# Two products per weight load: ordering the wq and w3 products so that the second reuses what the first has loaded

## Chip, cores, metric

The kernel runs on one core of a Trainium2 chip. The metric is device time in microseconds (us) of one execution. Times of the two kernels are compared over fast runs of the same rounds; "same" means within 2%.

## The reference, cut to what matters

One decode step of two blocks on the same token, summed: attention over a cached K and V (32 query heads, 4 KV heads, 65,536 positions, head size 128), and a small MLP mixer. All inputs are bfloat16.

```python
xn = layernorm(A_x)                                  # 1 x 1024
q = xn @ A_wq                                        # wq: 1024 x 4096
p = softmax(q @ k_cache.T * 128**-0.5); o = p @ v_cache   # 8 query heads share one KV head
h = gelu(layernorm(xn) @ w1); x1 = xn + shift(h) @ w2
h2 = gelu(layernorm(x1) @ w3) @ w4                   # w3: 1024 x 3584
out = A_x + o @ A_wo + x1 + h2
```

K and V alone are 134 MB of the 170 MB that the kernel reads, once each.

## The kernel before

Everything arrives through one DMA queue, issued by SyncE, into three slots of SBUF. First wq (slot 0), w1 and w2 (slot 1), w3 (slot 2); then K and V in eight blocks of 8.4 MB each. K block m goes to slot 0 or 2, V blocks always to slot 1. A load can be issued only when the slot's last reader is done, so three of these issues hang on the first 70 us of compute:

```python
issue(3)   # K block 0 into slot 0: after the q products have read wq
...
issue(4)   # V block 0 into slot 1: after the w1 and w2 products
...
issue(5)   # K block 1 into slot 2: after w3's products and the gelu
...
issue(6 + 2*m)   # V block m+1 into slot 1: after block m's last P*V product
```

The products that the change touches have a stationary operand of 32 equal columns (one column of the vector, broadcast) and a moving operand of 512 weights. The array of TensorE is used as four column tiles of 32 columns, each writing its own 32 partitions of PSUM, so four products can run at once (in the trace of before they start in fours, the first four within 0.01 us). For one j all four tiles hold the same column of the vector:

```python
for j in range(KT_D):               # 8 slices of the 1024 inputs
    for b in range(2):              # two PSUM banks
        for jj in range(4):         # four column tiles
            fns.append(lambda e, j=j, b=b, jj=jj: e.matmul(
                S_ps[32 * jj:32 * jj + 32, b, :], xn_bf[:, j:j + 1].broadcast_to([P, 32]),
                KV[:, 0, j * HQD + 512 * (4 * b + jj):j * HQD + 512 * (4 * b + jj + 1)],
                start=(j == 0), stop=(j == KT_D - 1), tile_position=(0, 32 * jj)))
_grp(q_pe, fns, reads=b_KV[0] + [b_xn], writes=[b_S[0], b_S[1]])
issue(3)
```

That is 64 products (line L379 of the profile), each with a weight load of its own (PEld). The same for w3 inside `proj` (line L411, third part): 56 products, seven per j, tile `k % 4`. Both stages are 16 *steps* if four products always run together: 64/4, and two steps for the seven of each j.

Of the kernel before, what the change touches and what calls it, by code (L numbers as in the profile page):

```python
# [6 lines left out]
BF = mybir.dt.bfloat16  # L7
# [109 lines left out]
def _op(q, fn, reads=(), writes=(), partial=False, loop=False):  # L117
    _deps(q, reads, writes)
    ev = q.op(fn, True, loop)
    _done(ev, reads, writes, partial)  # L120
    return ev


def _grp(q, fns, reads=(), writes=(), partial=False):
    _deps(q, reads, writes)
    ev = None
    for i, fn in enumerate(fns):
        ev = q.op(fn, i == len(fns) - 1)
    _done(ev, reads, writes, partial)
    return ev  # L130
# [16 lines left out]
def bass_parallel_sum__gqa_block_cached__mixer_s_mlp__decode_kernel(  # L147
# [31 lines left out]
    with ExitStack() as es:  # L179
# [194 lines left out]

        fns = []
        for j in range(KT_D):
            for b in range(2):
                for jj in range(4):
                    fns.append(lambda e, j=j, b=b, jj=jj: e.matmul(  # L379
                        S_ps[32 * jj:32 * jj + 32, b, :], xn_bf[:, j:j + 1].broadcast_to([P, 32]),  # L380
                        KV[:, 0, j * HQD + 512 * (4 * b + jj):j * HQD + 512 * (4 * b + jj + 1)],
                        start=(j == 0), stop=(j == KT_D - 1), tile_position=(0, 32 * jj)))
# [21 lines left out]
        def proj(s, o, ncol, vec, bank, reads, c0):  # L404
            nper = ncol // P
            nt = nper // 4
            fns = []
            for j in range(KT_D):
                for k in range(nt):
                    mv = bass.AP(KV[:].tensor, s * SLOT + o + j * ncol + 4 * k, [[kvstep, P], [nper, P], [1, 4]])  # L410
                    fns.append(lambda e, j=j, k=k, mv=mv: e.matmul(  # L411
                        S_ps[32 * (k % 4):32 * (k % 4) + 32, bank + k // 4, :], vec[:, j:j + 1].broadcast_to([P, 32]), mv,
                        start=(j == 0), stop=(j == KT_D - 1), tile_position=(0, 32 * (k % 4))))
            nbank = (nt + 3) // 4
            _grp(q_pe, fns, reads=reads, writes=b_S[bank:bank + nbank])
            for b in range(nbank):
                nb = min(4, nt - 4 * b)
                if b == 0:
                    _op(q_dve, lambda e, b=b, nb=nb: e.tensor_copy(pT_f[0:32 * nb, b, :], S_ps[0:32 * nb, bank + b, :]), reads=[b_S[bank + b]], writes=[b_pT[b]])  # L419
                else:  # L420
                    _op(q_act, lambda e, b=b, nb=nb: e.activation(pT_f[0:32 * nb, b, :], S_ps[0:32 * nb, bank + b, :], ACTF.Copy), reads=[b_S[bank + b]], writes=[b_pT[b]])
            fns = []
            for b in range(nbank):
                nb = min(4, nt - 4 * b)
                for c in range(4):
                    fns.append(lambda e, b=b, nb=nb, c=c: e.matmul(  # L426
                        M_ps[:, c0 + 16 * b + c:c0 + 16 * b + 4 * nb:4], pT_f[0:32 * nb, b, c:512:4], ident_f[0:32 * nb, 0:32 * nb:32],
                        start=(b + c == 0), stop=True, skip_group_check=True))
            _grp(q_pe, fns, reads=b_pT[0:nbank] + [b_const], writes=[b_M])

        def gelu(src_ps, width, dst_bf, b_src, b_dst):
# [7 lines left out]
            _op(q_dve, lambda e: e.tensor_tensor(out=dst_bf, in0=a_, in1=xs_, op=ALU.mult), reads=[b_misc], writes=[b_dst])  # L439

        proj(1, 0, D, xn2_bf, 2, b_w1 + [b_xn2], 256)
        gelu(M_ps[:, 256:256 + KT_D], KT_D, h1g_bf, b_M, b_h1)
        proj(1, 8 * D, D, g_bf, 3, b_w2 + [b_const], 272)
        _op(q_dve, lambda e: e.tensor_tensor(out=x1, in0=xn, in1=M_ps[:, 272:272 + KT_D], op=ALU.add), reads=[b_xn, b_M], writes=[b_x1])
        _op(q_dve, lambda e: e.tensor_tensor(out=acc[:], in0=acc[:], in1=M_ps[:, 272:272 + KT_D], op=ALU.add), reads=[b_acc, b_M], writes=[b_acc])
        issue(4)
        layer_norm(x1, b_x1, xn3, xn3_bf, b_xn3, 208)
        proj(2, 0, F, xn3_bf, 0, b_KV[2] + [b_xn3], 288)
        gelu(M_ps[:, 288:288 + KT_F], KT_F, gh_bf[:], b_M, b_gh)
        q_sp.wait_all([(q.sem, q.cnt) for q in (q_pe, q_dve, q_act, q_pool)])  # L450
# [200 lines left out]
        code = nc.m.functions[0].blocks[0].instructions  # L651
# [48 lines left out]
                nc.tensor.wait_ge(s_, v).then_inc(s_, -v)  # L700
        q_pe.emit(nc.tensor, q_pe.ops[marks[-1]:])


# [1 line left out]
_INS = ['A_x', 'A_k_cache', 'A_v_cache', 'A_wq', 'A_wo', 'B_x', 'B_w1', 'B_w2', 'B_w3', 'B_w4']  # L705
# [24 lines left out]
```

## Time and profile before

| | before |
|---|---|
| time, median of 6 runs | 400.44 us (400.36 to 400.53) |
| weight loads / products on TensorE | 1539 / 1539 |
| data queue's share of the 16 DMA engines' span | 98.7% |
| q products start, result read | 27.66, 34.21 us |
| w3 products start, result read | 58.93, 65.21 us |
| block 0 begins (first transpose of K) | 71.50 us |
| V block 1 issued / K block 1 landed | 101.21 / 108.6 us |

From the page of the kernel before: busy time per engine; the data queue (packets, MB, share of 16 engines' span); and the chain that ended last, by engine.

```profile
PE 177.8 (45%) x1539; PEld 61.1 (15%) x1539; DVE 221.3 (55%) x260; ACT 23.9 (6%) x50; POOL 7.7 (2%) x31
...
q1 hardware_dynamic: 3608, 169.87, 98.7%
...
DMA 58%; DVE 25%; PE 14%; issue 1%; ACT 1%; SPq 1%; POOL 0%
```

No compute engine is busy for much more than half of the span; the DMA engines are hardly ever idle. The next lines are the same chain in order of time (start, length, what).

```profile
27.66 6.53 PE S_ps L379 x63
...
58.93 6.26 PE S_ps L411 x43
...
71.52 37.07 DMA KV<-in_A_k_cache_dram
108.61 13.10 DVE KV L460 x3
```

The two stages that change are on the chain, but only before 71.5 us. From there on, the chain is mostly K loads and the transposes that wait for them, with w4's load at the end. The first question for such a change is therefore whether a stage before 71.5 us can move anything after it. The timeline, cut to its first 3.4 us of q products and to the end of block 0, shows the steps and the DMA issue that matters (start, length, engine; SPq is the issue itself):

```profile
27.66 0.14 PEld L379 LDWEIGHTS S_ps<-KV 128*32 128x32 bf16 x8 [1.45 <-DVE KV L359]
27.66 3.60 PE L379 MATMUL S_ps<-KV 128*32 128x512 bf16 x32 [1.36 <-DVE KV L359]
28.07 0.16 PEld L379 LDWEIGHTS S_ps<-KV 128*32 128x32 bf16 x4 [0.27 <-issue]
28.49 0.16 PEld L379 LDWEIGHTS S_ps<-KV 128*32 128x32 bf16 x4 [0.27 <-issue]
...
101.21 0.33 SPq L290 DMA_DIRECT2D KV<-in_A_v_cache_dram  x1
...
108.61 4.45 DVE L460 STREAM_TRANSPOSE KV<-KV 128x4096 f32<-128x4096 f32 x1 [6.43 <-DMA KV<-in_A_k_cache_dram]
```

Four loads every 0.43 us, always under the products of the step before. V block 1 is issued 7.4 us before K block 1 has wholly landed.

### The profile page before, as it was taken

Reading aid. Unit: us, or ns where it says so; the run is one execution under the profiler, and the core shown is the slowest. Engines: PE = TensorE matmul, PEld = TensorE weight load, DVE = VectorE, ACT = ScalarE, POOL = GpSimd, SP = SyncE. Lnnn points to the kernel's source line nnn. Section 1 sums busy time; section 2 is a strip of 40 time slices with the busy share of each in tenths; the row PEclk is TensorE's granted clock in tenths of the full one; section 3 lists DMA queues with packets and bytes.
Section 4 is the critical chain, followed back from the end, with each engine's and each line's share of the span. In section 5 each row is a group of like instructions: output and inputs, shape, how many; then the busy total and the mean of one; then the engine's idle time right before and its main releaser. Section 6 shows DMA issues by size and latency. Waiting matters only on the chain.

```text
span 399.3 us, 3500 instructions
## 1 busy us (share of the span) xinstructions
PE 177.8 (45%) x1539; PEld 61.1 (15%) x1539; DVE 221.3 (55%) x260; ACT 23.9 (6%) x50; POOL 7.7 (2%) x31
## 2 busy tenths in 40 slices
PE   0035669147134713560358036413661462147394
PEld 0022435012001110110012001100120110012232
DVE  0024230995298539843984597269647952895201
ACT  1000000011001100110011002000100110011000
POOL 5000000000000000000000000000000000000000
PEclk9998656555755665585557555855565558555979
DMA  9999899999999999999999999999999999999995
GB/s 420 420 387 487 382 441 479 440 415 427 415 427 427 433 474 433 420 427 420 433 427 433 473 433 420 421 420 433 433 433 473 433 420 420 420 433 433 416 424 219
DMA packets 3759, 169.97 MB, mean 426 GB/s; under 512 B 548, under 2 KB 552, under 8 KB 808
## 3 DMA queue, kind: packets, MB, share of 16 engines
q1 hardware_dynamic: 3608, 169.87, 98.7%
q8 instruction: 5, 0.08, 0.1%
q10 hardware_dynamic: 144, 0.00, 0.0%
q14 instruction: 2, 0.02, 0.0%
HBM read 169.87 MB, written 0.00 MB: 425 GB/s over the span
## 4 chain that ended last, share of the span: by engine, by line
DMA 58%; DVE 25%; PE 14%; issue 1%; ACT 1%; SPq 1%; POOL 0%
DMA KV<-in_A_k_cache_dram 44%; DVE KV L460 17%; DMA KV<-in_B_w_dram 8%; DMA KV<-in_A_x_dram 6%; PE S_ps L411 3%; PE OT_ps L518 3%; DVE mrow L481 2%; PE M_ps L426 2%; PE S_ps L474 2%; PE S_ps L379 2%; ACT p_sb L496 1%; DVE Yall L395 1%; PE PT_ps L505 1%; DVE pT_f L509 1%; DVE pT_f L419 1%
## 5 line engine op out<-in xcount | busy, mean ns | idle before, releaser
L460 DVE STREAM_TRANSPOSE KV<-KV 128x4096 f32<-128x4096 f32 x32 | 140.3, 4421 | 42.2 <-DMA KV<-in_A_k_cache_dram 42.2
L474 PE MATMUL S_ps<-KV,Ycur 128*32 128x512 bf16 x512 | 60.7, 623 | 126.1 <-DVE KV L460 126.1
L518 PE MATMUL OT_ps<-KV,pT_f 128*32 128x512 bf16 x512 | 46.6, 504 | 1.2 <-DVE pT_f L509 1.2
L474 PEld LDWEIGHTS S_ps<-KV,Ycur 128*32 128x32 bf16 x512 | 14.3, 126 | 158.1 <-DVE KV L460 140.5
L496 ACT ACTIVATE p_sb<-S_ps,brun 128x1024 bf16<-128x1024 f32 x16 | 17.8, 1114 | 274.7 <-DVE brun L494 174.3
L509 DVE STREAM_TRANSPOSE pT_f<-PT_ps 128x512 f32<-128x512 f32 x32 | 22.4, 701 | 14.0 <-PE PT_ps L505 14.0
L481 DVE TENSOR_REDUCE mrow<-S_ps 128x1 f32<-128x1024 f32 x16 | 19.3, 1204 | 11.3 <-PE S_ps L474 11.3
L484 PE MATMUL M_ps<-Rm,Lmat 128*128 128x16 bf16 x16 | 3.1, 194 | 38.0 <-DVE Rm L482 38.0
L505 PE MATMUL PT_ps<-p_sb,permR 128*128 128x512 bf16 x32 | 18.3, 573 | 0.8
L529 DVE SCALAR_TENSOR_TENSOR O_acc<-O_acc,ff,OT_ps 128x512 f32<-128x512 f32 x12 | 9.0, 747 | 14.4 <-PE OT_ps L518 14.4
L518 PEld LDWEIGHTS OT_ps<-KV,pT_f 128*32 128x32 bf16 x512 | 12.9, 114 | 23.6 <-issue 15.5
L411 PE MATMUL S_ps<-KV 128*32 128x512 bf16 x88 | 12.5, 571 | 2.7 <-DVE KV L359 2.7
L339 DVE CAST KV<-KV 128x8 f32<-128x8 bf16 x1 | 0.2, 172 | 22.4 <-DMA KV<-in_A_x_dram 22.4
L578 PE MATMUL S_ps<-KV,o_bf 128*1 128x512 bf16 x64 | 9.7, 476 | 4.8 <-DMA KV<-in_A_wo_dram 4.8
L484 PEld LDWEIGHTS M_ps<-Rm,Lmat 128*128 128x128 bf16 x16 | 1.7, 104 | 49.3 <-DVE Rm L482 49.3
L426 PE MATMUL M_ps<-ident_f,pT_f 64*128 64x2 f32 (+2 forms) x32 | 7.9, 372 | 2.4 <-DVE pT_f L419 2.4
L582 DVE COPY pT_f<-S_ps 1x512 f32<-1x512 f32 x1 | 0.7, 679 | 14.4 <-PE S_ps L578 14.4
L426 PEld LDWEIGHTS M_ps<-ident_f,pT_f 64*128 64x128 f32 (+2 forms) x32 | 7.7, 326 | 4.7 <-DVE pT_f L419 3.4
L419 DVE COPY pT_f<-S_ps 64x512 f32<-64x512 f32 (+1 forms) x3 | 2.1, 685 | 11.3 <-PE S_ps L411 11.3
L505 PEld LDWEIGHTS PT_ps<-p_sb,permR 128*128 128x128 bf16 x32 | 3.3, 102 | 27.2 <-ACT p_sb L496 14.7
L364 PE MATMUL M_ps<-KV 8*128 8x8 bf16 x1 | 0.2, 182 | 16.2 <-DVE Dmat_f L363 16.2
L379 PE MATMUL S_ps<-KV 128*32 128x512 bf16 x64 | 6.5, 593 | 1.4 <-DVE KV L359 1.4
(88 smaller groups left out, 88.8 us busy)
## 6 DMA issues: line engine op xcount, KB each, us to landing
KV<-in_B_w_dram SPq DMA_DIRECT2D x1, 7168.0 KB, 48.4
KV<-in_B_w_dram SPq DMA_DIRECT2D x1, 4352.0 KB, 27.4
KV<-in_B_w_dram SPq DMA_DIRECT2D x2, 2048.0 KB, 28.4
KV<-in_B_w_dram SPq DMA_DIRECT2D x1, 1792.0 KB, 31.4
KV<-in_B_w_dram SPq DMA_DIRECT2D x1, 768.0 KB, 32.8
KV<-in_B_w_dram SPq DMA_DIRECT2D x1, 256.0 KB, 32.9
KV<-in_A_k_cache_dram SPq DMA_DIRECT2D x8, 46.5
KV<-in_A_v_cache_dram SPq DMA_DIRECT2D x8, 28.0
```

Of the source, the lines that this page charges most:

```text
L379: fns.append(lambda e, j=j, b=b, jj=jj: e.matmul(S_ps[32 * jj:32 * jj + 32, b, :], xn_bf[:, j:j + 1].broadcast_to([P, 32]), KV[:, 0, j * H ...
L411: fns.append(lambda e, j=j, k=k, mv=mv: e.matmul(S_ps[32 * (k % 4):32 * (k % 4) + 32, bank + k // 4, :], vec[:, j:j + 1].broadcast_to([P, ...
L426: fns.append(lambda e, b=b, nb=nb, c=c: e.matmul(M_ps[:, c0 + 16 * b + c:c0 + 16 * b + 4 * nb:4], pT_f[0:32 * nb, b, c:512:4], ident_f[0:3 ...
L460: _op(q_dve, lambda e: e.transpose(out=KV32[:, s, o:o + 4096], in_=KV32[:, s, o:o + 4096]), reads=[b_KV[s][sub]], writes=[b_KV[s][sub]], l ...
L474: fns.append(lambda e, we=we, cm=cm, mv=mv: e.matmul(S_ps[32 * cm:32 * cm + 32, n % 4, :], Ycur[:, we, :, :].rearrange("p a g -> p (a g)") ...
L481: _op(q_dve, lambda e: e.reduce_max(mrow[:, k:k + 1], S_ps[:, 2 * k:2 * k + 2, :].rearrange("p b c -> p (b c)"), axis=AX.X), reads=b_S[2 * ...
L496: _op(q_act, lambda e: e.activation(p_sb[:, :, :].rearrange("p b c -> p (b c)"), S_ps[:, 2 * k:2 * k + 2, :].rearrange("p b c -> p (b c)") ...
L505: _op(q_pe, lambda e: e.matmul(PT_ps[:, :], permR[:, :], p_sb[:, n % 2, :], start=True, stop=True), reads=[b_p[n % 2], b_const], writes=[b ...
L509: _op(q_dve, lambda e: e.transpose(out=pT_f[:, n % 2, :], in_=PT_ps[:, :]), reads=[b_PT], writes=[b_pT[n % 2]], loop=True)
L518: fns.append(lambda e, q=q, q4=q4: e.matmul(OT_ps[32 * q4:32 * q4 + 32, g % 2, :], pT_bf[:, n % 2, q, :, 1], KV[:, s, 8192 * sub + 512 * q ...
L529: _op(q_dve, lambda e: e.scalar_tensor_tensor(out=O_acc[:, 0:512], in0=O_acc[:, 0:512], scalar=ff[:, k:k + 1], in1=OT_ps[:, k, :], op0=ALU ...
L578: _grp(q_pe, [lambda e, j=j, jj=jj: e.matmul(S_ps[32 * jj:32 * jj + 1, 1, :], o_bf[:, j:j + 1], KV[:, 0, j * D + 512 * jj:j * D + 512 * (j ...
```

## The change

Two products that use the same weights on the same column tile are made neighbours, and the second is issued without a load of its own.

```diff
         for j in range(KT_D):
-            for b in range(2):
-                for jj in range(4):
+            for jj in range(4):
+                for b in range(2):
                     fns.append(lambda e, j=j, b=b, jj=jj: e.matmul(
@@ proj: w1, w2, w3
-                for k in range(nt):
+                for k in sorted(range(nt), key=lambda k: (k % 4, k)):
@@ after the program has been emitted
+        prev, n_ld = None, 0
+        for k, i in enumerate(code):
+            if i.opcode != "Matmult":
+                continue
+            key = (i.tile_position, i.tile_size, str(i.ins[1].memref), i.ins[1].offset, str(i.ins[1].ap))
+            if key == prev and i.ins[1].dtype == BF and not i.sync_info:
+                code[k] = mybir.InstMatmult(... (cut: the same operands) ..., ldweights=False)
+                n_ld += 1
+            prev = key
+        assert n_ld > 40, n_ld
```

For q the order of tiles goes from 0 1 2 3 0 1 2 3 to 0 0 1 1 2 2 3 3; for w3 from 0 1 2 3 0 1 2 to 0 0 1 1 2 2 3. w1 and w2 have two products per j, on different tiles, and do not change. 55 loads go: 31 of q (the last product carries a semaphore and keeps its load) and 24 of w3.

## The prediction

> **What bounds the kernel now.** DMA. The queue table gives the load queue 98.7% of 16 engines' span; 169.9 MB move at 425 GB/s. The chain of waits is 58% DMA, and from 71.5 us on it runs through the K loads: the first transposes of each later block (L460) wait for a K load (42 us in all). Only before 71.5 us are the q and w3 products on a chain of compute: q products (L379) 27.66 to 34.2, w3 products (L411) 58.93 to 65.2. Even there the DMA queue stays full, because loads are issued far ahead: K block 1, issued at 71.52, starts moving only when V block 0 has landed (89).

> **What the change removes.** 55 of 1539 weight loads. One lasts about 0.146 us, but the timeline shows them running under matmuls: four matmuls start together every 0.427 us, with four loads inside. Nothing is waited for; the gain is about 0 us.

> **What it adds.** The four column tiles run at once: 64 q products take 16 steps of 0.427 us (0.216 when the clock is full), not 64. The new order puts two products of one tile in succession. They cannot overlap[...], so only the second product of one tile and the first of the next run together: two at once, not four. Weight loads still get pulled ahead ([...]the trace agrees: eight loads in the first 0.14 us, four of them past waiting matmuls).
> - q: 33 steps instead of 16. The clock rises to full at 33.5 us in this trace; 14 cold steps, then 0.216 each: end near 37.9, +3.7 us.
> - between: w1 and w2 keep their order; their luck with the clock moves, +0.3 to +1.0 us.
> - w3: three steps per j instead of two, 25 for 16: 7.9 us for 6.3, +1.7 us.
> Sum: block 0 starts near 77.2 instead of 71.5, +5.7 us (estimate, +-1 with the phase of the clock, whose full and half periods are multiples of 3.41 us in the records).

> **How much is critical.** K block 0 issue moves 34.2 to 37.9; the queue has work until 50. K block 1 issue moves to 77.2; work until 89. Both absorbed. The tight one is V block 1, issued when block 0's last PV products end: 101.2, now near 107.0 to 107.5. K block 1 lands on the first DMA engines at 106.3 and on the last at 108.6. The first load shows about 1.0 us from issue to first packet and a first packet 0.8 us longer than the later 2.42 us. So most engines idle 1 to 3 us, and the last, which sets the end, 0 to 1 us. Afterwards each later issue again has over 5 us of room. This bubble is never made up: +0.2 to +1.8 us at the end.

> **Prediction.** 401.2 us, 8 in 10 within 400.3 to 402.8. Faster by over 2%: 0.01; within 2%: 0.97; slower by over 2%: 0.02.

> **What would show it.** PEld count 1484. L379 lasts about 10 us, matmuls in pairs; L411's third part about 8. Block 0's first transpose near 77; V block 1 issued near 107; a dip of DMA share near 107 to 109, and K block 2 landing 0.3 to 2 us later than 147.3. Block 1's start stays at 108.6. If no dip: 400.4.

> **What would make it wrong.** If a weight load cannot pass the second product of the previous pair, each step grows by about 0.1 us, block 0 slips some 11 us, and the bubble reaches 5 us (406). If a tile accepted its second product without waiting, nothing moves. If the DMA engines' lags even out differently, the bubble counts fully (+2 to +3 us).

The premise of "two at once, not four" was that products start in program order. No trace shows the premise; it was an assumption of mine. Block 0's +5.7 us is +3.7 for q, +1.7 for w3 and +0.3, the low end of what stands for w1 and w2.

## The result, and the profile after

| | before | after |
|---|---|---|
| time, median of 6 runs | 400.44 us (400.36 to 400.53) | 400.48 us (400.33 to 400.66) |
| weight loads / products recorded | 1539 / 1539 | 1484 / 1523 |
| q: start, result read, length | 27.66, 34.21, 6.55 us | 27.53, 32.58, 5.05 us |
| w3: start, result read, length | 58.93, 65.21, 6.28 us | 57.91, 63.16, 5.25 us |
| block 0 begins | 71.50 us | 69.50 us |
| V block 1 issued / K block 1 landed | 101.21 / 108.6 us | 99.84 / 108.2 us |

The ratio is 1.0001, interval 0.9988 to 1.0014: the same. The 16 products that after lacks are missing from the trace, not from the program: they are of L505, which the page of after counts 16 times instead of 32. All 64 of L379 and all 88 of L411 are there.

The chain of after, in order of time, with the lines that answer to those above:

```profile
27.53 5.03 PE S_ps L379 x64
...
57.91 5.23 PE S_ps L411 x34
...
69.47 38.72 DMA KV<-in_A_k_cache_dram
108.21 13.10 DVE KV L460 x3
```

Both stages got *shorter*, not longer, and the wait for K block 1 that follows took up nearly all of it: 38.72 us for 37.07. The timeline of after:

```profile
27.53 0.12 PEld L379 LDWEIGHTS S_ps<-KV 128*32 128x32 bf16 x4 [1.45 <-DVE KV L359]
27.53 3.69 PE L379 MATMUL S_ps<-KV 128*32 128x512 bf16 x40 [1.36 <-DVE KV L359]
27.93 0.16 PEld L379 LDWEIGHTS S_ps<-KV 128*32 128x32 bf16 x4 [0.28 <-issue]
28.78 0.16 PEld L379 LDWEIGHTS S_ps<-KV 128*32 128x32 bf16 x4 [0.69 <-issue]
29.64 0.16 PEld L379 LDWEIGHTS S_ps<-KV 128*32 128x32 bf16 x4 [0.69 <-issue]
30.40 0.11 PEld L379 LDWEIGHTS S_ps<-KV 128*32 128x32 bf16 x4 [0.60 <-issue]
...
99.84 0.33 SPq L290 DMA_DIRECT2D KV<-in_A_v_cache_dram  x1
```

Four loads now come every second step: 27.93 to 28.78 is 0.85 us, two times 0.427. Half of the loads are gone, and the length of a step is what it was. The start of every single product is in the trace (us; "+" marks one beside which a load starts, within 5 ns):

```
before  27.663+ 27.667+ 27.670+ 27.673+ | 28.065+ 28.068+ 28.072+ 28.074+ | 28.492+ 28.494+ 28.498+ 28.501+
after   27.530+ 27.535+ 27.540+ 27.545+ | 27.929+ 27.935+ 27.941+ 27.946+ | 28.355  28.362  28.368  28.373
```

This was not in the prediction: four start together, although the program says tile 0, tile 0, tile 1, tile 1. A load that starts beside a product is mostly not that product's own, but one pulled ahead for the tile's next weights. In before the first group has eight loads, four of its own and four (27.677 to 27.687 us) for the second group; three of these four have passed a product that still waits (the prediction says four). In after the second group are the second products of the four tiles, which have no loads of their own: the loads at 27.93 are for the next j, whose products are the third group. e2 below shows the same on one tile alone, with a load beside every second product. (The trace does not name the tile of a product. That the four are of four tiles follows from e2 too, where products of one tile never start closer than one step, 0.427 us before the clock goes up and 0.216 us after it.)

Why was the stage 1.5 us shorter, then? Count the steps in the trace: 16 in both kernels, for q and for w3 alike. What differs is when the granted clock went up (in w3 of before the record has 0.50 up to 64.21 us and 1.00 from there, and the steps go from 0.427 to 0.219 us): steps of 0.427 us become steps of 0.216 us at 33.49 us in the trace of before, 5.83 us after the first product, and at 30.30 us, 2.77 us after it, in that of after. The experiments show the same relation (table under e1), and a check there says that it is not the change.

### The profile page after: what moved, and what is told of

It reads as the page before. It is cut to its first block, busy times and chain, and to the rows that moved or that the text cites. A ratio compares the mean times of both kernels' runs of the same rounds, so it can differ in the third digit from the quotient of the medians.

```text
span 399.1 us, 3429 instructions
## 1 busy us (share of the span) xinstructions
PE 168.9 (42%) x1523; PEld 59.0 (15%) x1484; DVE 221.4 (55%) x260; ACT 23.9 (6%) x50; POOL 7.7 (2%) x31
## 3 DMA queue, kind: packets, MB, share of 16 engines
q1 hardware_dynamic: 3608, 169.87, 98.7%
## 4 chain that ended last, share of the span: by engine, by line
DMA 59%; DVE 25%; PE 12%; issue 1%; ACT 1%; SPq 1%; POOL 0%
DMA KV<-in_A_k_cache_dram 45%; DVE KV L460 18%; DMA KV<-in_B_w_dram 8%; DMA KV<-in_A_x_dram 6%; PE S_ps L411 3%; PE OT_ps L518 2%; DVE mrow L481 2%; PE M_ps L426 2%; PE S_ps L474 2%; PE S_ps L379 1%; ACT p_sb L496 1%; DVE Yall L395 1%; DVE pT_f L509 1%; DVE pT_f L419 1%; PE PT_ps L505 0%
## 5 line engine op out<-in xcount | busy, mean ns | idle before, releaser
L460 DVE STREAM_TRANSPOSE KV<-KV 128x4096 f32<-128x4096 f32 x32 | 140.3, 4422 | 44.3 <-DMA KV<-in_A_k_cache_dram 44.3
L411 PE MATMUL S_ps<-KV 128*32 128x512 bf16 x88 | 12.1, 538 | 2.7 <-DVE KV L359 2.7
L505 PE MATMUL PT_ps<-p_sb,permR 128*128 128x512 bf16 x16 | 9.7, 607 | 0.8
L505 PEld LDWEIGHTS PT_ps<-p_sb,permR 128*128 128x128 bf16 x32 | 3.3, 102 | 27.5 <-ACT p_sb L496 14.7
```

What stands on the lines that cost most here:

```text
L411: fns.append(lambda e, j=j, k=k, mv=mv: e.matmul(S_ps[32 * (k % 4):32 * (k % 4) + 32, bank + k // 4, :], vec[:, j:j + 1].broadcast_to([P, ...
L460: _op(q_dve, lambda e: e.transpose(out=KV32[:, s, o:o + 4096], in_=KV32[:, s, o:o + 4096]), reads=[b_KV[s][sub]], writes=[b_KV[s][sub]], l ...
L505: _op(q_pe, lambda e: e.matmul(PT_ps[:, :], permR[:, :], p_sb[:, n % 2, :], start=True, stop=True), reads=[b_p[n % 2], b_const], writes=[b ...
```

## The experiments

Theory A: a load costs nothing because it runs under the products in flight, and a product that waits for its own tile does not hold back the other tiles; and what happens before block 0 moves the end only when V block 1 is issued too late. Rivals: B, products start strictly in program order (the assumption behind the prediction); C, loads do cost, and either the new order hides it or the room before the DMA does. All eleven kernels of the experiments gave the correct result.

### e1: the new order, all loads kept

```diff
 (the change's two new orders stay)
-        prev, n_ld = None, 0
-        for k, i in enumerate(code): ... ldweights=False
```

> The order of the change, with every weight load kept. Theory A (loads lie hidden under the four products in flight, and a product that waits for its own column tile does not hold back the products of other tiles): the q products start four together, every 0.427 us with the half clock and every 0.216 us with the full clock, 64 loads, and the time is 400.4 +-0.3 us, as before and as with the change. Theory B (my prediction: products start strictly in program order): pairs of two, 33 steps. Theory C (the removed loads are what kept the changed order from costing time): with the loads back, the steps grow above 0.427 and 0.216 us.

Measured: 400.51 us, ratio 1.0000 (0.9984 to 1.0017). All 64 loads are there, eight in the first step and four in each later one but the last, and the 64 products go in 16 steps of 0.427 and 0.216 us. A holds; B falls; C in the form "the missing loads pay for the order" falls.

With the length of q set beside the moment at which the steps change from 0.427 to 0.216 us (both from the trace), five kernels fall on one line. With T the time from the first product to that moment, 16 steps take T + (16 - T/0.427) x 0.216, and about 0.2 us pass from the end of the last step to the reader (0.22 in before, 0.24 in after):

| kernel | loads of q | T, us | by the formula | q length, us |
|---|---|---|---|---|
| after | 33 | 2.77 | 5.0 | 5.05 |
| e1, new order, all loads | 64 | 3.35 | 5.3 | 5.35 |
| e4, old order, half the loads | 33 | 4.58 | 5.9 | 5.93 |
| before | 64 | 5.83 | 6.5 | 6.55 |
| e3, runs of four, half the loads | 33 | 5.95 | 6.6 | 6.67 |

The formula is an estimate from the two step lengths. Neither the number of loads nor the order appears in it. Whether they move T itself has to be asked: in the three runs with q in pairs T was short (2.77, 3.35 and 3.65 us in after, e1 and r8_after), and in the four with q in the old order long (4.58 to 5.83 us in e4, r2, r8_before and before). The w3 stage answers it: in pairs and with the same loads left out, its clock went up 3.11 us after its first product in after and 5.29 us in e3; in the old order of before it was 5.28 us. So one order has both, and the short times of q in pairs are chance as far as these traces show. In the traces of before and after the granted clock goes to and fro between 1.00 and 0.50, and each whole stretch lasts 1 to 10 times 3.41 us (before: 1.00 from 33.49 to 36.90, 0.50 to 47.14, 1.00 to 50.56, 0.50 to 64.21 us). The rise in q came at no fixed time from the kernel's start: 30.30 us in after, 30.96 in e1, 31.95 in e4, 33.44 in e3, 33.49 in before (first product plus T). Here that makes 1.6 us of difference between stages that do the same (5.05 to 6.67 us). A stage comparison on one profile each would have credited the change with it.

### e2: sixteen in a row on one tile

```diff
-        for j in range(KT_D):
-            for jj in range(4):
+        for jj in range(4):
+            for j in range(KT_D):
                 for b in range(2):
```

> The q products ordered tile by tile: sixteen in a row on one column tile (eight weights, each used twice), then the next tile. Counts steps of one product time. Theory A with a short queue for each tile (depth d of products waiting): about 16 + 3 x (15 - d) steps, so about 58 for d = 1, 46 for d = 5. Theory A without a limit: 16 steps, four together from the start. Theory B (strict program order): about 61 steps, hardly ever two at once.

Measured: 49 steps; q took 13.17 us; 403.43 us (one look; before, on the same chip, 400.39 to 400.66). Loads of q in the timeline, from the start and from where the second tile joins:

```profile
27.37 0.10 PEld L379 LDWEIGHTS S_ps<-KV 128*32 128x32 bf16 x1 [1.45 <-DVE KV L359]
27.77 0.15 PEld L379 LDWEIGHTS S_ps<-KV 128*32 128x32 bf16 x1 [0.30 <-issue]
28.63 0.15 PEld L379 LDWEIGHTS S_ps<-KV 128*32 128x32 bf16 x1 [0.70 <-issue]
...
31.19 0.15 PEld L379 LDWEIGHTS S_ps<-KV 128*32 128x32 bf16 x1 [0.70 <-issue]
32.04 0.81 PEld L379 LDWEIGHTS S_ps<-KV 128*32 128x32 bf16 x5 [0.70 <-issue]
33.19 0.10 PEld L379 LDWEIGHTS S_ps<-KV 128*32 128x32 bf16 x1 [0.34 <-issue]
```

The starts of the products show 11 steps with one product each, then 5 steps with two, then 6 with one, 5 with two, and so on. So products of one tile go one at a time, and the next tile begins when the one before it has four products still waiting: 16 + 3 x 11 = 49. The order does matter; it only has to be much worse than that of the change.

This run also tests the other half of the prediction, because it delays everything by as much as I had predicted for the change: block 0 begins at 77.59 us and V block 1 is issued at 107.01 (predicted: near 77.2, and 107.0 to 107.5). The DMA view between 104 and 112 us, first of before, then of e2, there with the issue of V block 1 from its timeline:

```profile
DMA packets 65, 3.21 MB, mean 401 GB/s; under 512 B 16, under 2 KB 16, under 8 KB 16
...
q1 hardware_dynamic: 65, 3.21, 93.3%
```

```profile
107.01 0.33 SPq L290 DMA_DIRECT2D KV<-in_A_v_cache_dram  x1
...
DMA packets 51, 2.29 MB, mean 287 GB/s; under 512 B 16, under 2 KB 16, under 8 KB 16
...
q1 hardware_dynamic: 51, 2.29, 73.9%
```

There is the bubble: by the trace's DMA packets the 16 engines idle about 1.9 us in the mean between 100 and 113 us, and 0.0 us in before. K block 1 lands on time (108.05) and block 1 begins on time, but V block 1 lands at 130.0 instead of 127.9 and everything behind it stays late. The time grew by 2.95 us over the 400.48 of before (one look). The prediction's mechanism for a late issue is right; its size, +0.2 to +1.8 us, was too small, and the case it listed under what would make it wrong ("the bubble counts fully (+2 to +3 us)") is what happened.

### e3: runs of four on one tile

```diff
-        for j in range(KT_D):
-            for jj in range(4):
+        for j0, jj, dj in [(j0, jj, dj) for j0 in range(0, KT_D, 2) for jj in range(4) for dj in range(2)]:
+            for j in [j0 + dj]:
                 for b in range(2):
```

> The q products in runs of four on one column tile (two j, each twice). If one waiting product per tile is all that can be held (d = 1): about 34 steps in place of 16, two tiles at a time. If d is 3 or more: 16 steps, as before. Strict program order: about 49 steps.

Measured: 16 steps, four products together from the first on; 400.38 us (one look). In its first step nine products of tiles 0 to 2 wait while tile 3's first product has already started. So the limit seen in e2 is not on all waiting products together but on those of one tile. Its trace happens to have the clock of before (T 5.95 us), and then all its times agree with before's: block 0 begins at 71.47 us for 71.50.

### e5 and e6: runs of eight, with and without the loads

e5 is e3 with groups of four j in place of two (runs of eight); e6 is e5 without the part that drops loads.

> The q products in runs of eight on one tile. If each tile holds four waiting products (as the 49 = 16 + 3 x 11 steps of runs of sixteen suggest): the next tile starts three steps after the last, 29 steps in all, at most three tiles at once. If only the total of waiting products were limited, runs of four would not have gone four at a time.

> Runs of eight on one tile with every load kept. If a tile's queue holds four products whatever loads stand between them: 29 steps, as e5_run8 should. If loads take up places in it: fewer products wait, and more steps: 37 where only two products wait (starts five steps apart).

### e4: the old order, loads left out all the same

```diff
 (the order of before)
+        held = {}            # weights that each column tile holds
+        ...
+            if held.get(i.tile_position) == key and i.ins[1].dtype == BF and not i.sync_info:
+                code[k] = ... ldweights=False
+            held[i.tile_position] = key
```

> The order of before, but the second product of each column tile and weights (four products later in the program) has its load left out, since the tile should still hold the weights: 54 loads fewer without any change of order. If each column tile keeps its own weights, the result is correct and the time 400.4 +-0.3 us, steps 0.427 and 0.216. If a load for one tile disturbs what the others hold, the result is wrong.

Measured: correct, 400.42 us, ratio 1.0000 (0.9983 to 1.0017), 16 steps, 33 loads in q. So the change's new order is not even needed to drop the loads. The expectation took this for a test of whether a tile keeps its weights while others are loaded. It is a weak one, because the three loads in between bring the same column of the vector, and a weight overwritten by them could not be told from one that was kept. e2 is stronger: a load of the second tile, of another column, starts within 3 ns of one of the first (32.041 and 32.044 us), the first tile then does two products with one load, and the result was correct.

### r8: the same stage where nothing hides it

The q products eight times over (the last result stands), in the order of before and as changed:

```diff
-        _grp(q_pe, fns, reads=b_KV[0] + [b_xn], writes=[b_S[0], b_S[1]])
+        _grp(q_pe, 8 * fns, reads=b_KV[0] + [b_xn], writes=[b_S[0], b_S[1]])
```

> The order of before, the q products done eight times over (the last result stands): 128 steps and 512 loads. Theory A: 0.216 us a step with the full clock, the stage about 29 to 30.5 us for 6.5, so later starts move by about 24 us, more than the room there is, and the time grows to about 419 +-2 us. So here the q products are on the path, and r8_after shows what the change does there.

> The change, q products eight times over: 128 steps, 256 loads fewer. Theory A (the removed loads were hidden, and the order costs nothing): same steps of 0.427 and 0.216 us and the same time as r8_before to within 0.3%. Rival (a load costs something that one pass is too short to show, or that the room before the DMA covers): 256 loads at 0.01 us or more would make it 2.5 us or more faster than r8_before.

Measured: 420.69 us (419.24 to 420.79) and 419.94 us (419.79 to 420.68); ratios to before 1.0498 (1.0484 to 1.0513) and 1.0493 (1.0479 to 1.0507). The stage is on the path now: what precedes block 0 is worth 20 us. The groups of line L379, r8_before first, then r8_after (busy us, mean ns):

```profile
L379 PE MATMUL S_ps<-KV 128*32 128x512 bf16 x512 | 30.4, 403 | 1.4 <-DVE KV L359 1.4
L379 PEld LDWEIGHTS S_ps<-KV 128*32 128x32 bf16 x512 | 13.8, 102 | 17.5 <-issue 3.2 <-DVE KV L359 1.4
```

```profile
L379 PE MATMUL S_ps<-KV 128*32 128x512 bf16 x512 | 29.6, 396 | 1.4 <-DVE KV L359 1.4
L379 PEld LDWEIGHTS S_ps<-KV 128*32 128x32 bf16 x257 | 7.1, 100 | 23.5 <-issue 21.9 <-DVE KV L359 1.4
```

The 0.8 us between 30.4 and 29.6 are the clock again: 13 steps up to the change of the clock in the one, 9 in the other (the last of them already shortened), and 4 x (0.427 - 0.216) is 0.84. With the full clock the mean step is 24.606/114 = 0.2158 us with all loads (from the start of step 14 to that of step 128) and 25.470/118 = 0.2158 us with half of them (from step 10). 255 loads fewer save nothing that can be seen. This settles C: the zero is not hidden by the room before the DMA.

### r2: how much room there is

The q products twice over in the order of before (`2 * fns`).

> The order of before, q products done twice: a delay of about 3.5 us and nothing else. V block 1 is then issued near 103.5 to 104.7, before the first DMA engine runs dry near 106.2 less about 1 us: the time stays 400.4 +-0.3. With runs of sixteen the issue came at 107.0 and the time grew by 2.95 us.

Measured: 401.31 us (one look; before 400.21 to 400.65 on that chip), so about +0.9 us, where I expected none. V block 1 was issued at 103.84 us, inside the expected range; the engines idled about 0.3 us in the mean, and V block 1 landed at 128.4. Put in order of the issue of V block 1, all single runs but the first (s64_held is described below; its stage was longer for another reason):

| kernel | V block 1 issued, us | from K block 1 wholly landed to V block 1 wholly landed, us | time, us |
|---|---|---|---|
| before | 101.21 | 19.4 | 400.44 |
| e5 | 102.82 | 19.4 | 400.50 |
| r2 | 103.84 | 20.3 | 401.31 |
| e6 | 104.35 | 20.9 | 403.21 |
| s64_held | 104.65 | 21.1 | 402.98 |
| e2 | 107.01 | 21.9 | 403.43 |

The first engine runs out of K block 1 at about 106.2 us (first landing 106.28 in before, 106.25 in after). A load issued 3.4 us earlier (e5) came in time, with 19.4 us in the third column as in before; one issued 2.4 us earlier (r2) did not, with 20.3. I had allowed 1.0 us, taken from the start of the kernel. The third column grows smoothly; the last does not: e6 and s64_held lost about a further microsecond after V block 1. In e6 it was in the last loads, where one of the last w4 parts landed on its last engine 4.2 us after its first, instead of 2.3. s64_held shows 4.2 us there too, but had lost its microsecond before that (V blocks landed 1.5 us later than in before at 245.6 us and 2.5 us later at 285.3). Why is open in both.

### s64: products an eighth as long

To find where a load would cost time, each q product is cut into eight of 64 columns; the order is that of before. `s64_held` also leaves out the loads that a tile does not need, as e4 does.

```diff
-            for b in range(2):
+            for b, c in [(b, c) for b in range(2) for c in range(8)]:
                 for jj in range(4):
-                        S_ps[32 * jj:32 * jj + 32, b, :], ...
+                        S_ps[32 * jj:32 * jj + 32, b, 64 * c:64 * c + 64], ... (and the same 64 of KV)
```

> The order of before with each q product cut into eight of 64 columns: 512 products and 512 loads in 128 steps. If loads stay hidden however short the products: 0.053 us a step with the half clock, 0.027 with the full one, the stage about as long as before, 5 to 6.5 us. If a load becomes the limit when it takes longer than the products beside it (eight loads took 0.14 us at the start of the stage): 0.07 us a step or more, the stage about 9 us.

> The same 64-column products, a load only where a tile's weights change (32 for the q products instead of 512). If loads are what limits s64_loads: steps of 0.053 and 0.027 us and a stage of 5 to 7 us, shorter than with the loads by 2 us or more. If both have the same length, something else (the issue of a product) limits, and even here the removal of loads buys nothing.

Measured: 412.14 and 402.98 us (one look each; before 400.14). Loads cost a great deal here, but not as either branch of the expectation had it. With all 512 loads the steps are still 0.053 and 0.029 us, the same as without. What the stage loses are holes. First the products of s64_loads, then of s64_held (start, length, count, idle before):

```profile
27.49 2.78 PE L379 MATMUL S_ps<-KV 128*32 128x64 bf16 x216 [1.36 <-DVE KV L359]
35.42 1.90 PE L379 MATMUL S_ps<-KV 128*32 128x64 bf16 x128 [5.15 <-issue]
41.89 1.90 PE L379 MATMUL S_ps<-KV 128*32 128x64 bf16 x128 [4.57 <-issue]
48.36 0.73 PE L379 MATMUL S_ps<-KV 128*32 128x64 bf16 x40 [4.57 <-issue]
```

```profile
27.74 4.93 PE L379 MATMUL S_ps<-KV 128*32 128x64 bf16 x404 [1.36 <-DVE KV L359]
35.63 1.60 PE L379 MATMUL S_ps<-KV 128*32 128x64 bf16 x108 [2.96 <-issue]
```

128 products with 128 loads are 256 instructions. The trace has instruction packets of 16,384 bytes on a DMA queue of their own, at 33.06, 39.54 and 46.03 us in s64_loads, each about 1.1 us long, and the products go on 1.2 to 1.3 us after each has ended (35.42, 41.89, 48.36). My reading, from these times and counts alone, is that each packet brings the next 256 instructions; the trace does not name what a packet holds. Every hole of s64_loads cost 4.57 us or more: 256 short instructions took 1.9 us, and a packet came only every 6.5 us. s64_held has one hole, of 2.96 us, instead of three. In both runs the first hole comes after 432 instructions: 216 products and 216 loads, or 404 products and 28 loads. So a dropped load was worth something here, where TensorE stood idle between these packets, and by that count what it was worth is the place of one instruction. Why a packet came only every 6.5 us was not shown.

## Why the prediction came out as it did

The measured time, 400.48 us, lies in the stated range, at its lower end; the prediction's own reason for a number above 400.4 did not occur.

- *"What the change removes: the gain is about 0 us."* Right, and shown three ways: e1 has all loads and the same steps; e4 drops half of them without any new order; r8 has 0.2158 us a step with and without.
- *"They cannot overlap"* (two products of one tile). Right: e2 has 11 steps with one product each.
- *"so only the second product of one tile and the first of the next run together: two at once, not four"*. This is the step that failed. I had assumed that products start strictly in program order across column tiles, which no trace had shown. The trace of after shows four products starting within 0.02 us in an order of tiles 0 0 1 1 2 2 3 3, and runs of four still go four at a time (e3, 16 steps). Only longer runs lose (with half the loads, 29 steps at eight and 49 at sixteen).
- *"q: 33 steps instead of 16"* and *"25 for 16"* for w3: 16 and 16.
- *"block 0 starts near 77.2 instead of 71.5"*: it began at 69.50. The step count did not change, and the granted clock went up earlier: 2.77 us after the first product for 5.83 in q, 3.11 for 5.28 in w3, by chance as far as the traces show.
- *"How much is critical"*: the absorbed delays and the tight one were named rightly; e2 set the delay that I had predicted (107.01) and it cost 2.95 us, not 0.2 to 1.8. I had counted 1.0 us from issue to first packet; in r2 a load issued 2.4 us before the first engine ran dry already came late, and the time grew by about 0.9 us (one look).
- *"If a tile accepted its second product without waiting, nothing moves"* and *"If no dip: 400.4"*: in substance what happened. The second product is taken in and waits, without holding back the rest (four starts within 0.02 us).

So the range held by luck as much as by reasoning. The stages kept their step count, so the path after block 0 was never put to the test. Had they grown as I predicted, the time would, by e2 (one look), have been near 403.4 us, above the range: there the DMA queue absorbed only about half of the 6.1 us delay of block 0. The center of 401.2 rested on a delay that does not exist, and my price for that delay was too low as well; with the first error, the second did not show.

## What to carry to other kernels

Before removing weight loads, look at the step length, not at the busy time of the loads: loads that run under the products in flight cost nothing here (r8: 0.2158 us a step with 512 loads and with 257), and what mattered, by the fit and the counts above, was the places that they take as instructions: with very short products (s64: three holes with 512 loads, one with 33), or with a long run on one tile (e6: 36 steps with all loads, 29 in e5 with half). Column tiles forgave an order in which the same tile came two or four times in a row (16 steps), but not eight or sixteen (29 and 49 steps with half the loads). Compare stages by the count and length of their steps; the length of a stage in one profile also contains the moment at which the granted clock goes up, worth 1.6 us here (5.05 to 6.67 us for the same 16 steps).
